# First group of heads taken in pairs, with TensorE's order there written out

## The chip, the cores and the metric

The kernel runs on one core of one Trainium2 chip. The metric is device microseconds (us) of one execution; the median of three runs of the kernel before is 717.41 us (717.05 to 717.48).

## The reference, cut to what matters

Causal attention with a bias from cumulative sums, then a mixture of four experts over every token, then a gated feed-forward layer. All inputs are fp32.

```
scores = q k^T / 8 ;  cum = cumsum(max(s, 0))
scores = where(causal, -1e9, scores + min(cum_k - cum_q, 0))
attn = exp(scores - max) ;  x = (attn @ v) / (sum(attn) + 1e-9)      # 2 batches, 8 heads, 576 rows, 64 wide
p = probs / (sum(probs) + 1e-9) ;  y = sum_e p_e * relu(x @ w1_e) @ w2_e   # 1152 tokens, 512 wide, 4 experts, 1024 inner
out = ((y @ w_a) * (y @ w_b)) @ w_out                                 # 1536 inner
```

## The kernel before, in words

Attention is cut into four groups of query rows, each over all eight heads. The **first group** is the first 256 rows of batch 0 and runs alone at the start, in plain fp32, by the functions `head_scores`, `head_softmax`, `head_turn`, `head_av` and `pair_out`. Its output, turned so that model columns lie on partitions (`x32`, four pieces, one for each pair of heads), feeds the first matmuls of the first expert (`ps1`, line L1055, made of four products each, one for each piece). From there on TensorE mixes expert matmuls with the attention of groups two to four (jobs; their score matmuls are lines L631 and L632, their transposes L674).

In the first group q and k of an even head lie on partitions 0 to 63 and those of the odd head on 64 to 127 (tile `qk`); the bias rows (`cb`, a rounded part in 8 rows and its remainder 32 rows further on) are kept twice, from partition 0 and from partition 64. So the score matmuls of an even head use array rows 0 to 63 and those of an odd head rows 64 to 127. The scores of a head are two blocks, 128 queries over 128 keys and 128 queries over 256 keys; each block is a bias product (`one`, `rows`) and a q k product in one PSUM tile `sc`, of which there are two. Then VectorE (DVE) takes the minimum and writes `e` (five buffers of tag "e"; the first three of them hold `s_sb`, `ones` and `dif` of the cumulative sums at the start), ScalarE (ACT) exponentiates, TensorE turns `e` in three transposes into `tr`, ACT (even heads) or DVE (odd heads) copies that to `eT`, TensorE multiplies by v with a column of ones (`av`, one tile for a pair), DVE divides (`l`, `r`, `xq`), TensorE turns the pair's result (`xT`), and ACT writes `x32` and `xh`, GpSimd (POOL) `xl`.

The order of instructions on an engine is the scheduler's, except where `in_order` fixes it. `keep_warm(n)` issues n filler matmuls (bf16, 128x512, tile `lull`) with a fixed place. The first job's q, k and v are prepared by `prep_job` behind the third pair (`gate`): ACT writes `qh` and `ks` (L597, L602), SyncE's queue (SP) copies the upper half of `ks` into `kb` by DMA (L603), and POOL writes the remainder into the lower half of `ks` (L605). POOL also forms the experts' shares from `pr`, which SP loads late (`den`, L906 and L908).

Of the kernel before, what the change touches and what calls it, by code (L numbers as in the profile page):

```python
# [8 lines left out]
F32 = mybir.dt.float32  # L9
# [8 lines left out]
B, H, S, D = 2, 8, 576, 64  # L18
E, DM, F1, F2 = 4, 512, 1024, 1536
NT = B * S  # L20
P = 128
# [31 lines left out]
NB = 32 + H  # L53
NS = 64 + NB
# [5 lines left out]
def fused_kernel(ctx, tc, qk0, v0, qT, kT, v, s, dp, w1, w2, wa, wb, wo, out):  # L60
    nc = tc.nc
# [13 lines left out]
    ident = const.tile([P, P], F32, name="ident")  # L75
# [458 lines left out]
    ps_s = actx.enter_context(tc.tile_pool(name="ps_s", bufs=2, space=PSUM))  # L534
# [19 lines left out]
    def in_order(ins):  # L554
        return tc.keep_in_program_order(ins)

    qk = slab.tile([P, H // 2, 2, NT0], F32, tag="wh", name="qk")
# [9 lines left out]
    cb = slab.tile([NS, NT0], F32R, tag="wl", name="cb")  # L567
# [169 lines left out]
    def keep_warm(n):  # L737

        for _ in range(n):
            in_order(nc.tensor.matmul(lull_ps, lhsT=lull[:, :P], rhs=lull, start=True, stop=True))  # L740

    sc = e_p.tile([NS, S], F32, tag="e", name="s_sb")
# [4 lines left out]
    sel = fix_p.tile([NS, H], F32R, name="sel")  # L747
# [34 lines left out]
    in_order(nc.vector.tensor_scalar(  # L782
        out=cb, in0=cum[:NS, :NT0], scalar1=1.0, scalar2=1.0, op0=ALU.mult, op1=ALU.mult
    ))
    for lo_, eng in ((slice(32, NB), nc.vector), (slice(96, NS), nc.gpsimd)):
        in_order(eng.tensor_tensor(
            out=cb[lo_], in0=cum[lo_, :NT0], in1=cb[lo_].bitcast(F32), op=ALU.subtract
        ))
    nc.gpsimd.memset(v65[:, :, :, D : D + 1], 1.0)

    K0 = 3 * P
    heads = {}

    def head_scores(h):
        a = (h % 2) * D
        q, k = (qk[a : a + D, h // 2, i] for i in range(2))
        one, rows = sel[a : a + NB, h : h + 1].broadcast_to([NB, P]), cb[a : a + NB]
        ps = ps_s.tile([P, K0], F32, tag="sc", name=f"sc{h}")
        heads[h] = {"ps": ps}
        for n0, n1, q0 in ((0, P, 0), (P, K0, P)):  # L800
            nc.tensor.matmul(
                ps[:, n0:n1], lhsT=one, rhs=rows[:, : n1 - n0], start=True, stop=False
            )
            nc.tensor.matmul(  # L804
                ps[:, n0:n1], lhsT=q[:, q0 : q0 + P], rhs=k[:, : n1 - n0], start=False, stop=True
            )
        if h % 2:
            keep_warm(1)

    def head_softmax(h):  # L810
        ps = heads[h]["ps"]
        e = heads[h]["e"] = e_p.tile([P, K0], F32, tag="e", name=f"e{h}")
        mn = st_p.tile([P, 2], F32, tag="mn", name="mn")
        for i, (n0, n1) in enumerate(((0, P), (P, K0))):
            nc.vector.tensor_tensor_reduce(
                out=e[:, n0:n1], in0=ps[:, n0:n1], in1=causal[:, S - n1 + n0 :],
                scale=-SCALE, scalar=3.0e38, op0=ALU.add, op1=ALU.min, accum_out=mn[:, i : i + 1],
            )
            nc.scalar.activation(
                out=e[:, n0:n1], in_=e[:, n0:n1], func=AF.Exp, bias=mn[:, i : i + 1], scale=-1.0  # L820
            )

    def head_turn(h):
        e = heads[h]["e"]
        ps = ps_t.tile([P, 3, P], F32, tag="tr", name=f"tr{h}")
        for i in range(3):
            nc.tensor.transpose(ps[:, i, :], e[:, i * P : i * P + P], ident)
        eT = heads[h]["eT"] = et_p.tile([P, 3, P], F32, tag="eh", name=f"eT{h}")
        if h % 2:
            nc.vector.tensor_copy(out=eT, in_=ps)  # L830
        else:
            nc.scalar.activation(out=eT, in_=ps, func=AF.Copy)

    def head_av(h):
        eT = heads[h]["eT"]
        if h % 2 == 0:
            heads["av"] = ps_m.tile([P, 2, 2, VW], F32, tag="mm", name="av0")
        av = heads["av"]
        for t, i, c, first_, last in ((0, 0, 0, True, True), (1, 1, 0, True, False), (1, 2, 1, False, True)):
            nc.tensor.matmul(  # L840
                av[:, t, h % 2, : D + 1], lhsT=eT[:, i, :], rhs=v65[:, c, h, : D + 1],
                start=first_, stop=last,
            )
        if h % 2:
            keep_warm(1)

    last = []

    def pair_out(j):
        av = heads["av"]  # L850
        l, r = (st_p.tile([P, 2, 2], F32, tag=t, name=t) for t in "lr")
        nc.vector.tensor_scalar(out=l, in0=av[:, :, :, D], scalar1=1e-9, scalar2=None, op0=ALU.add)
        nc.vector.reciprocal(out=r, in_=l)
        xq = x_p.tile([P, 2, 2, D], F32, tag=("xs", "xt")[j % 2], name="xq")
        x = nc.vector.tensor_tensor(
            out=xq, in0=av[:, :, :, :D], in1=r.unsqueeze(3).broadcast_to([P, 2, 2, D]), op=ALU.mult
        )
        ps = ps_a.tile([P, NT0], F32, tag="av", name="xT")
        for t in range(2):
            nc.tensor.transpose(  # L860
                ps[:, t * P : t * P + P], xq[:, t].rearrange("p a d -> p (a d)"), ident
            )
        y = nc.scalar.activation(out=x32[j], in_=ps, func=AF.Copy)
        last.append((x.ins, y.ins))
        nc.scalar.activation(out=xh[j][:, :NT0], in_=ps, func=AF.Copy)
        nc.gpsimd.tensor_tensor(
            out=xl[j][:, :NT0], in0=x32[j], in1=xh[j][:, :NT0].bitcast(F32), op=ALU.subtract
        )
# [42 lines left out]
        for e in range(E):  # L911
            nc.gpsimd.tensor_tensor(out=pr[:, :, e], in0=pr[:, :, e], in1=den, op=ALU.mult)

    for h in range(H + 3):
        if h < H:
            head_scores(h)
        if h == 0:
            sums_of_s()
        if h < H:
            head_softmax(h)  # L920
        if 0 <= h - 2 < H:
            head_turn(h - 2)
        if 0 <= h - 3 < H:
            head_av(h - 3)
            if (h - 3) % 2:
                pair_out((h - 3) // 2)

    jobs = [make_job(gi, h) for gi in range(1, len(GROUPS)) for h in range(H)]

# [4 lines left out]
    def at(n):  # L934
        return seq[n] if 0 <= n < len(seq) else None
# [364 lines left out]
    for n in range(len(seq) + 12):  # L1300
        x = at(n)
# [108 lines left out]
```

## Time and profile before

| what | value |
|---|---|
| median of three runs | 717.41 us |
| the profiled execution: its own time | 716.52 us |
| the profiled execution: span of its instructions | 714.8 us |
| PE busy / DVE / ACT / POOL in that span | 707.0 / 500.2 / 334.0 / 419.7 us |

The span runs from the first to the last instruction of the trace; 1.7 us of the execution lie outside it. A busy PE in this profile has modelled ends, so the starts of its instructions tell more than its share.

### The profile page before, as it was taken

What the parts mean: (1) busy time and instruction counts of PE and PEld (TensorE: products, weight loads), DVE (VectorE), ACT (ScalarE), POOL (GpSimd) and SP (SyncE); (2) the same over time, 40 slices, a digit from 0 to 9 for tenths busy, and PEclk for the clock granted to TensorE, in tenths of its full rate; (3) what the DMA queues carried; (4) which work ended last, traced back from release to release, by engine and by line L of the source; (5) the groups of instructions that cost most, each with busy time, mean ns of one, the idle gap of its engine ahead of it and who ended that gap; (6) DMA issues with size and microseconds to landing.
All of it is one profiled execution on the core that took longest, in us unless ns stands there. A gap on an engine that the chain in (4) does not pass through costs nothing.

```text
span 714.8 us, 11136 instructions
## 1 busy us (share of the span) xinstructions
PE 707.0 (99%) x3892; PEld 621.7 (87%) x3892; DVE 500.2 (70%) x1039; ACT 334.0 (47%) x734; POOL 419.7 (59%) x421
## 2 busy tenths in 40 slices
PE   9999999999999999999999999999999999999998
PEld 5877899999999988888888888887999899989886
DVE  5567978877769576667666666588976557875672
ACT  3568969988743333333333223434543544423410
POOL 5476876766623564444344357578275898878700
PEclk9999999999999999999999999999999999999999
DMA  8665742454211121222111131222021322222002
GB/s 327 202 192 151 224 129 84 107 142 113 74 59 41 60 88 37 68 62 71 53 53 56 47 88 61 88 87 91 30 72 47 98 82 88 86 66 85 30 30 104
DMA packets 34877, 65.63 MB, mean 92 GB/s; under 512 B 3413, under 2 KB 17653, under 8 KB 34821
## 3 DMA queue, kind: packets, MB, share of 16 engines
q1 hardware_dynamic: 34341, 63.81, 28.7%
q10 hardware_dynamic: 480, 1.11, 0.4%
q8 instruction: 31, 0.51, 0.3%
q14 instruction: 25, 0.20, 0.1%
HBM read 59.31 MB, written 2.58 MB: 87 GB/s over the span
## 4 chain that ended last, share of the span: by engine, by line
PE 89%; POOL 3%; DVE 3%; DMA 2%; ACT 2%; issue 1%; ACTq 0%; DVEq 0%; POOLq 0%
PE ps L284 39%; PE psq L284 30%; PE pst L284 6%; PE ps L1055 3%; PE av L706 3%; PE tr L674 3%; POOL wl L84 2%; PE sc L632 1%; PE sc L631 1%; PE sc L804 1%; PE av L840 1%; DMA qk<-in_qk 1%; PE psq L1160 1%; POOL tp L165 1%; DMA raw<-in_w 1%
## 5 line engine op out<-in xcount | busy, mean ns | idle before, releaser
L284 PE MATMUL ps<-wh,h2h 128*128 128x512 f32 (+1 forms) x320 | 124.8, 390 | 0.0
L284 PE MATMUL ps<-wl,h2h 128*128 128x512 f32 (+1 forms) x320 | 123.9, 387 | 0.0
L284 PE MATMUL ps<-wh,h2l 128*128 128x512 f32 (+1 forms) x320 | 122.1, 388 | 0.0
L84 POOL TENSOR_TENSOR wl<-raw,wh 128x512 fp32r<-128x512 f32 x48 | 62.2, 1322 | 101.5 <-ACT wh L80 80.7
L338 DVE SCALAR_TENSOR_TENSOR acc<-ps,pr,acc 128x512 f32<-128x512 f32 x105 | 77.6, 746 | 38.5 <-PE ps L284 38.0
L284 PE MATMUL psq<-xh,wh 128*128 128x448 f32 (+1 forms) x224 | 81.5, 365 | 0.8 <-DVE psq L439 0.8
L284 PE MATMUL psq<-xl,wh 128*128 128x448 f32 (+1 forms) x224 | 81.3, 363 | 0.0
L284 PE MATMUL psq<-xh,wl 128*128 128x448 f32 (+1 forms) x224 | 81.3, 364 | 0.0
L349 ACT ACTIVATE h2h<-psq 128x448 fp32r<-128x448 f32 (+1 forms) x56 | 29.7, 531 | 102.5 <-PE psq L284 82.4
L284 PEld LDWEIGHTS ps<-wh,h2l 128*128 128x128 f32 x320 | 60.1, 188 | 12.5
L284 PEld LDWEIGHTS ps<-wh,h2h 128*128 128x128 f32 x320 | 60.2, 188 | 11.1 <-DVE acc L338 0.4
L284 PEld LDWEIGHTS ps<-wl,h2h 128*128 128x128 f32 x320 | 60.1, 188 | 10.7
L84 POOL TENSOR_TENSOR wl<-sums,wh 128x512 fp32r<-128x512 f32 x48 | 62.1, 1317 | 3.9 <-ACT wh L80 3.9
L284 PE MATMUL psq<-tql,wh 128*128 128x448 f32 x144 | 52.7, 366 | 0.0
L284 PE MATMUL psq<-tqh,wl 128*128 128x448 f32 x144 | 52.5, 364 | 0.0
L284 PE MATMUL psq<-tqh,wh 128*128 128x448 f32 x144 | 52.4, 365 | 0.0
L165 POOL TENSOR_SCALAR tp<-tp 128x512 f32<-128x512 f32 x24 | 46.9, 1968 | 5.3 <-ACT tp L164 5.3
L690 DVE TENSOR_TENSOR el<-tr,eh 128x512 fp32r<-128x512 f32 (+5 forms) x80 | 38.6, 485 | 14.0 <-ACT eh L689 12.9
L439 DVE TENSOR_TENSOR u<-psq,s 128x448 f32<-128x448 f32 x44 | 27.3, 620 | 29.8 <-PE psq L284 28.8
L663 POOL TENSOR_SCALAR e<-e,r 128x448 f32<-128x448 f32 (+4 forms) x64 | 37.9, 597 | 16.7 <-DVE r L662 11.4
L284 PEld LDWEIGHTS psq<-xh,wh 128*128 128x128 f32 x224 | 42.1, 188 | 4.7 <-DVE psq L439 1.1
L80 ACT ACTIVATE wh<-raw 128x1024 fp32r<-128x1024 f32 x24 | 25.5, 1062 | 43.6 <-PE ps L284 23.8
(204 smaller groups left out, 1931.5 us busy)
## 6 DMA issues: line engine op xcount, KB each, us to landing
raw<-in_w SPq DMA_DIRECT2D x40, 512.0 KB
raw<-in_wa SPq DMA_DIRECT2D x12, 512.0 KB
raw<-in_wb SPq DMA_DIRECT2D x12, 512.0 KB
raw<-in_wo SPq DMA_DIRECT2D x12, 512.0 KB
kr<-in_kT SPq DMA_DIRECT2D x16, 288.0 KB
w<-in_w SPq DMA_DIRECT2D x8, 512.0 KB
vr<-in_v SPq DMA_DIRECT2D x16, 160.0 KB
kb<-ks SPq DMA_DIRECT2D x16, 144.0 KB
```

The costliest lines, as they stand in the source:

```text
L80: nc.scalar.activation(out=hi, in_=src, func=AF.Copy)
L84: lo_eng.tensor_tensor(out=lo[:, x], in0=src[:, x], in1=hi[:, x].bitcast(F32), op=ALU.subtract)
L165: nc.gpsimd.tensor_scalar(out=t.bitcast(F32), in0=t.bitcast(F32), scalar1=2.0**-15, scalar2=GMAX, op0=ALU.max, op1=ALU.min,)
L284: ins = nc.tensor.matmul(ps, lhsT=l, rhs=r, start=first and k == 0, stop=last and k == 2, skip_group_check=more)
L338: nc.vector.scalar_tensor_tensor(out=dst, in0=ps, scalar=share, in1=dst, op0=ALU.mult, op1=ALU.add)
L349: nc.scalar.activation(out=hh, in_=src, func=AF.Relu)
L439: nc.vector.tensor_tensor(out=out, in0=a, in1=b, op=ALU.add)
L663: nc.gpsimd.tensor_scalar(out=t.e, in0=t.e, scalar1=r, scalar2=1.0, op0=ALU.mult, op1=ALU.mult)
L674: ins = nc.tensor.transpose(ps[:, c - c0, :], t.e[:, k0 : k0 + P], ident)
L690: nc.vector.tensor_tensor(out=j.el[:, c0:c1, x], in0=src, in1=hi.bitcast(F32), op=ALU.subtract)
L706: ins = nc.tensor.matmul(ps[:, o:], lhsT=j.vs[:, c, :], rhs=e[:, c, o:], start=(m == 0), stop=(m == len(mms) - 1),)
L1055: ins = nc.tensor.matmul(ps, lhsT=w, rhs=x, start=start, stop=stop)
```

## The change

`head_scores` now takes a pair of heads. It issues both bias products of a block, then both q k products, so that products of the even and the odd head follow one another on different array rows. Every TensorE instruction of the first group (scores, transposes, `av`, `xT`) is now fixed in program order. The fillers behind each pair's scores and behind each pair's `av` are gone (eight of them); three fillers stand behind the scores of the first pair. `pair_out` is split: `pair_norm` (the division, on DVE) comes right behind the pair's `av`, `pair_out` (the turn) one step later. The remainder of `cb` for odd heads moves from POOL to DVE.

```
-    for lo_, eng in ((slice(32, NB), nc.vector), (slice(96, NS), nc.gpsimd)):
-        in_order(eng.tensor_tensor(
+    for lo_ in (slice(32, NB), slice(96, NS)):
+        in_order(nc.vector.tensor_tensor(
...
-    def head_scores(h):
...
+    def head_scores(j):
+        two = []
+        for h in (2 * j, 2 * j + 1):
...
+            two.append((ps, q, k, one, rows))
         for n0, n1, q0 in ((0, P, 0), (P, K0, P)):
...
-        if h % 2:
-            keep_warm(1)
+            for ps, _, _, one, rows in two:
+                in_order(nc.tensor.matmul(
+                    ps[:, n0:n1], lhsT=one, rhs=rows[:, : n1 - n0], start=True, stop=False
+                ))
+            for ps, q, k, _, _ in two:
+                in_order(nc.tensor.matmul(
+                    ps[:, n0:n1], lhsT=q[:, q0 : q0 + P], rhs=k[:, : n1 - n0], start=False, stop=True
+                ))
...
-    for h in range(H + 3):
-        if h < H:
-            head_scores(h)
-        if h == 0:
+    NH = H // 2
+    for j in range(NH + 1):
+        if j < NH:
+            head_scores(j)
+        if j == 0:
+            keep_warm(3)
             sums_of_s()
-        if h < H:
-            head_softmax(h)
-        if 0 <= h - 2 < H:
-            head_turn(h - 2)
-        if 0 <= h - 3 < H:
-            head_av(h - 3)
-            if (h - 3) % 2:
-                pair_out((h - 3) // 2)
+        if j < NH:
+            head_softmax(2 * j)
+        if j:
+            head_turn(2 * j - 1)
+        if j > 1:
+            pair_out(j - 2)
+        if j < NH:
+            head_softmax(2 * j + 1)
+        if j:
+            head_av(2 * j - 2)
+            head_av(2 * j - 1)
+            pair_norm(j - 1)
+        if j < NH:
+            head_turn(2 * j)
+    pair_out(NH - 1)
```

The order of TensorE (PE) around the second pair, before. The number behind `sc`, `tr`, `e` and `eT` is the head, the rest of a name is a buffer number:

```order
L740 MATMUL lullps_122<-lull_120 128x512
L801 MATMUL sc2_225<-cb_114,sel_128 128x128
L804 MATMUL sc2_225<-qk_112 128x128
L801 MATMUL sc2_225<-cb_114,sel_128 128x256
L804 MATMUL sc2_225<-qk_112 128x256
L827 MATMUL tr0_236<-ident_71,e0_207 128x128 x3
L801 MATMUL sc3_242<-cb_114,sel_128 128x128
L804 MATMUL sc3_242<-qk_112 128x128
L801 MATMUL sc3_242<-cb_114,sel_128 128x256
L804 MATMUL sc3_242<-qk_112 128x256
L740 LDWEIGHTS lull_120
L740 MATMUL lullps_122<-lull_120 128x512
```

The same place on PE in the changed kernel:

```order
L831 MATMUL tr0_227<-ident_71,e0_215 128x128 x3
L806 MATMUL sc2_233<-cb_114,sel_128 128x128
L806 MATMUL sc3_234<-cb_114,sel_128 128x128
L810 MATMUL sc2_233<-qk_112 128x128
L810 MATMUL sc3_234<-qk_112 128x128
L806 MATMUL sc2_233<-cb_114,sel_128 128x256
L806 MATMUL sc3_234<-cb_114,sel_128 128x256
L810 MATMUL sc2_233<-qk_112 128x256
L810 MATMUL sc3_234<-qk_112 128x256
L831 MATMUL tr1_249<-ident_71,e1_221 128x128 x3
L844 MATMUL av0_261<-va_113,eT0_231 128x65 x3
L844 MATMUL av0_261<-va_113,eT1_253 128x65 x3
```

The two heads' scores stand together in turn, and the fillers and the transposes between them are gone.

The end of the first group on PE before, from the third pair's `xT` on (`ps1` are the expert's products, `sc0_0_2_2` and `sc0_0_2_3` the first job's first scores, `xT_416` the last pair's turn):

```order
L860 MATMUL xT_390<-ident_71,xq_388 128x128 x2
L1055 MATMUL ps1_465<-ckr_115,w32_116 128x256 x2
L840 MATMUL av0_402<-va_113,eT7_400 128x65 x3
L740 LDWEIGHTS lull_120
L740 MATMUL lullps_122<-lull_120 128x512
L1055 MATMUL ps1_465<-ckr_115,w32_116 128x256
L1055 MATMUL ps1_494<-ckr_115,w32_116 128x256 x3
L860 MATMUL xT_416<-ident_71,xq_414 128x128 x2
L1055 MATMUL ps1_501<-ckr_115,w32_116 128x256 x3
L631 MATMUL sc0_0_2_2_484<-ks0_0_2_442,qh0_0_2_422 128x320
L631 MATMUL sc0_0_2_3_503<-ks0_0_2_442,qh0_0_2_422 128x448
L632 MATMUL sc0_0_2_2_484<-kb0_0_2_425,qb1_84 128x320
```

The same place on PE in the changed kernel:

```order
L866 MATMUL xT_392<-ident_71,xq_378 128x128 x2
L844 MATMUL av0_398<-va_113,eT6_384 128x65 x3
L1070 MATMUL ps1_460<-ckr_115,w32_116 128x256 x2
L1070 MATMUL ps1_489<-ckr_115,w32_116 128x256 x2
L844 MATMUL av0_398<-va_113,eT7_390 128x65 x3
L1070 MATMUL ps1_460<-ckr_115,w32_116 128x256
L1070 MATMUL ps1_489<-ckr_115,w32_116 128x256
L631 MATMUL sc0_0_2_2_479<-ks0_0_2_437,qh0_0_2_417 128x320
L631 MATMUL sc0_0_2_3_498<-ks0_0_2_437,qh0_0_2_417 128x448
L632 MATMUL sc0_0_2_2_479<-kb0_0_2_420,qb1_84 128x320
L632 MATMUL sc0_0_2_3_498<-kb0_0_2_420,qb1_84 128x448
L866 MATMUL xT_411<-ident_71,xq_409 128x128 x2
```

Both have six products of the expert ahead of the last `xT` (twelve instructions in the trace, two for a product); but in the changed kernel the first job's four score matmuls stand ahead of that `xT`, and the three products of `ps1_496` behind it.

## Rows read from the trace of the kernel before

**Rows 1.** The page's line of TensorE: busy time (share of the span) xinstructions.

```profile
PE 707.0 (99%) x3892; PEld 621.7 (87%) x3892; DVE 500.2 (70%) x1039; ACT 334.0 (47%) x734; POOL 419.7 (59%) x421
```

**Rows 2.** Busy time by stretch (columns are length, busy us by engine, clock, DMA).

```profile
5.60:15.50 9.90, 9.61 (x59) 6.89 (x59) 4.75 (x22) 3.65 (x9) 5.54 (x6) 1.00 1.02 403
```

**Rows 3.** Timeline of PE, head 1 and a filler (start, length, engine, line).

```profile
6.95 0.32 PE L801 MATMUL sc<-cb,sel 40*128 40x128 f32 x1
...
8.03 0.39 PE L740 MATMUL lullps<-lull 128*128 128x512 bf16 x1
8.35 0.32 PE L801 MATMUL sc<-cb,sel 40*128 40x128 f32 x1
```

**Rows 4.** Timeline of PE, 20 to 32 us.

```profile
21.86 0.78 PE L840 MATMUL av<-va,eT 128*128 128x65 f32 x6
22.48 0.49 PE L827 MATMUL tr<-ident,e 128*128 128x128 f32 x3
22.81 0.38 PE L860 MATMUL xT<-ident,xq 128*128 128x128 f32 x2
...
28.50 0.38 PE L860 MATMUL xT<-ident,xq 128*128 128x128 f32 x2
28.71 1.46 PE L1055 MATMUL ps<-ckr,w 128*128 128x256 f32 x6
29.82 0.70 PE L631 MATMUL sc<-ks,qh 128*128 128x320 f32 x2
...
30.72 1.46 PE L1055 MATMUL ps<-ckr,w 128*128 128x256 f32 x6
```

**Rows 5.** Timeline of DVE, the first group (in brackets: idle before, and its releaser).

```profile
4.69 0.42 DVE L786 TENSOR_TENSOR cb<-va,cb 8x256 fp32r<-8x256 f32 x1
...
7.39 0.27 DVE L815 CUSTOM_DVE_ANT_0 e<-sc,causal 128x128 f32<-128x128 f32 x1
...
15.46 0.29 DVE L815 CUSTOM_DVE_ANT_0 e<-sc,causal 128x128 f32<-128x128 f32 x1 [3.15 <-POOL ckr L897]
...
16.02 0.29 DVE L815 CUSTOM_DVE_ANT_0 e<-sc,causal 128x128 f32<-128x128 f32 x1
...
17.32 0.55 DVE L830 COPY eT<-tr 128x384 f32<-128x384 f32 x1
```

**Rows 6.** Timeline of POOL, 4 to 34 us.

```profile
5.62 1.28 POOL L786 TENSOR_TENSOR cb<-va,cb 8x256 fp32r<-8x256 f32 x1
...
23.18 0.21 POOL L906 TENSOR_TENSOR den<-pr 128x9 f32<-128x9 f32 x1 [7.76 <-DMA pr<-in_dp]
...
23.93 1.42 POOL L866 TENSOR_TENSOR xl<-ckr,xh 128x256 fp32r<-128x256 f32 x2
...
27.05 1.55 POOL L605 TENSOR_TENSOR ks<-kr,ks 64x288 fp32r<-64x288 f32 x2 [0.30 <-POOL xl L866]
```

**Rows 7.** Timeline of SP's queue and of ACT: a DMA's issue, its reader.

```profile
27.59 0.52 SPq L590 DMA_DIRECT2D qr<-in_qT  x1
...
30.17 0.53 ACT L597 ACTIVATE qh<-qr 128x384 fp32r<-128x384 f32 x1 [0.24 <-DMA qr<-in_qT]
```

**Rows 8.** Busy time by stretch, 26 to 28 us (columns as in rows 2).

```profile
26.00:27.00 1.00, 1.00 (x10) 0.95 (x9) 0.62 (x1) 0.91 (x2) 0.73 (x1) 1.00 0.96 393
27.00:28.00 1.00, 1.00 (x6) 0.90 (x5) 0.93 (x5) 0.00 (x0) 0.95 (x2) 1.00 0.19 78
```

**Rows 9.** Timeline of PE, around its longest wait behind the first group.

```profile
82.75 0.38 PE L284 MATMUL ps<-xh,wh 128*128 128x256 f32 x1 [1.30 <-DVE hl L318]
82.97 0.28 PE L284 MATMUL ps<-xl,wh 128*128 128x256 f32 x1
83.09 0.28 PE L284 MATMUL ps<-xh,wl 128*128 128x256 f32 x1
```

**Rows 10.** Timeline of PE's weight loads, the fillers at the start.

```profile
3.91 0.15 PEld L740 LDWEIGHTS <-lull 128*128 128x128 bf16 x1 [0.28 <-issue]
4.34 0.82 PEld L740 LDWEIGHTS <-lull 128*128 128x128 bf16 x4 [0.28 <-issue]
```

More of the change, by code (lines that the diff above doesn't have):

```diff
@@ L792, in fused_kernel @@
     heads = {}
-    def head_scores(h):
[L795 to L799, printed above, removed]
-        for n0, n1, q0 in ((0, P, 0), (P, K0, P)):
[L801 to L806, printed above, removed]
-        if h % 2:
-            keep_warm(1)
+    def head_scores(j):
+        two = []
+        for h in (2 * j, 2 * j + 1):
+            a = (h % 2) * D
+            q, k = (qk[a : a + D, j, i] for i in range(2))
+            one, rows = sel[a : a + NB, h : h + 1].broadcast_to([NB, P]), cb[a : a + NB]
+            ps = ps_s.tile([P, K0], F32, tag="sc", name=f"sc{h}")
+            heads[h] = {"ps": ps}
+            two.append((ps, q, k, one, rows))
+        for n0, n1, q0 in ((0, P, 0), (P, K0, P)):
+            for ps, _, _, one, rows in two:
[6 more added lines that the diff above has]
+                ))
     def head_softmax(h):
@@ L826, in head_turn @@
         for i in range(3):
-            nc.tensor.transpose(ps[:, i, :], e[:, i * P : i * P + P], ident)
+            in_order(nc.tensor.transpose(ps[:, i, :], e[:, i * P : i * P + P], ident))
         eT = heads[h]["eT"] = et_p.tile([P, 3, P], F32, tag="eh", name=f"eT{h}")
@@ L839, in head_av, with pair_norm @@
         for t, i, c, first_, last in ((0, 0, 0, True, True), (1, 1, 0, True, False), (1, 2, 1, False, True)):
-            nc.tensor.matmul(
+            in_order(nc.tensor.matmul(
                 av[:, t, h % 2, : D + 1], lhsT=eT[:, i, :], rhs=v65[:, c, h, : D + 1],
                 start=first_, stop=last,
-            )
-        if h % 2:
-            keep_warm(1)
+            ))
     last = []
-    def pair_out(j):
+    def pair_norm(j):
         av = heads["av"]
@@ L857, in pair_out @@
         )
+        heads["x", j] = (x, xq)
+    def pair_out(j):
+        x, xq = heads["x", j]
         ps = ps_a.tile([P, NT0], F32, tag="av", name="xT")
         for t in range(2):
-            nc.tensor.transpose(
+            in_order(nc.tensor.transpose(
                 ps[:, t * P : t * P + P], xq[:, t].rearrange("p a d -> p (a d)"), ident
-            )
+            ))
         y = nc.scalar.activation(out=x32[j], in_=ps, func=AF.Copy)
```

## The prediction

> **What bounds the kernel now.** I read the page's line of engines first: TensorE (PE) is busy 707.0 of 714.8 us, the next engine 500.2 [rows 1]. So time can come only from PE's idle, from work that PE need not do, or from work that it does faster. The change touches PE up to the end of the first group alone; behind it the order of PE's instructions is the same list as before. So I looked for the row where both kernels have done the same PE work: the one after the last `xT`, six expert instructions and the first job's four score matmuls (two L631, two L632). In the kernel before that is 30.72 [rows 4]. PE is nearly full from there on, so what the change wins or loses at this point carries to the end, unless a later wait absorbs it.
>
> Then the timelines of that stretch. Between 5.60 and 15.50 PE counts as busy 9.61 of 9.90 us [rows 2], but that count holds modelled ends and fillers. From one start to the next, a head's four score instructions take 6.95 to 8.03, 1.08 us, and a filler 0.32 [rows 3]; a head's `av` takes 0.62 and its three transposes 0.33 (21.86, 22.48, 22.81), the last `xT` 0.21, six expert instructions 1.11 (28.71 to 29.82), and the four score products behind them 0.90 [rows 4]. DVE has a stall of 3.15 us in front of head 4's softmax, released by POOL at 15.46 [rows 5]. POOL is the engine to watch at the end of the group: it waits 7.76 us for the load of `pr`, forms `den` from 23.18, two `xl` from 23.93 (0.71 each), and ends with two L605 from 27.05, 1.55 together [rows 6]. L631 reads what L605 writes.
>
> **The change part by part.**
>
> *Fillers.* Eight go, three come: 5 x 0.32 = 1.6 us less of PE's issue [rows 3]. Some of those eight only filled waits, so 1.6 is an upper bound and 0 the lower.
>
> *Scores in turn.* A pair took 2 x 1.08 = 2.16 us [rows 3]. Nowhere in this trace do products of different array rows follow each other directly in a pair, so the price is unknown. The upper bound is serial: 0.32 + 0.76 a head, less one of the two exits to a full-array instruction, and I call that 2.0 (an estimate: the two heads with no other instruction between). The lower bound is one head's length, 1.08, with a little for issue: 1.2. The four pairs thus save between 0.6 and 3.8 us of PE time. I carry both ends and 1.5 between them. The page "TensorE: Matmul & The Clock Gate" of the Trainium skill, Part 3 (row/col tiling), says that matmuls on different row groups run at once and that weights load beside a running matmul only if the row group differs; by it the pair would be near 1.2. No row here shows this; by the sum below the end is the same at either price.
>
> *Remainder of `cb`.* DVE gets another instruction like the one at 4.69, 0.42 us [rows 5]; POOL loses one of 1.28 that began at 5.62 [rows 6], so that the odd head no longer waits for POOL until 6.9. DVE works without a gap towards head 0's softmax at 7.39 [rows 5], so that comes at about 7.8. With the exponentials behind it the first transposes come at about 8.9. Ahead of them PE has a pair of scores from 5.6 and three fillers (to 8.6 if serial, 7.8 if overlapped): an idle of up to 1.1 us where the kernel before had the next head's scores.
>
> *Order fixed in pairs.* PE now waits at each transposition for its own softmax. DVE needs 0.56 a head (15.46 to 16.02) and 0.55 for an `eT` copy [rows 5]. Walking the new order by hand with these durations, PE reaches:
>
> | PE comes to | serial 2.0 | half 1.5 | full 1.2 |
> |---|---|---|---|
> | the third pair's scores | 13.7 | 13.3 | 13.0 |
> | the transposes of head 5 | 20.1 | 19.1 | 18.8 |
> | the last `av` (head 7) | 25.7 | 24.8 | 24.5 |
> | L631, behind twelve expert instructions | 27.2 | 26.35 | 26.05 |
>
> These are estimates. Their check is simple: work from 5.6 on is 4 x 2.0 + 8 x 0.33 + 8 x 0.62 + 3 x 0.21 + 2 x 1.11 + 3 x 0.32 = 19.4 us if serial, which would end at 25.0; the other 2.2 us are waits for the softmax chain, half of them in the first pair. The softmax that waits for POOL until 15.46 is now that of head 5 instead of head 4 (the buffers' order moves by one), which comes later in the order and then costs little.
>
> *The end of the group.* In the new order the first job's L631 and L632 stand ahead of the last `xT`. So they have to wait for what they read, whatever the first group saved:
> - POOL: `pr` lands when it lands, 23.18, as its load does not depend on PE. From there `den` to 23.93, then three `xl` of 0.71 in place of two, to about 26.1, then L605 with 1.55: 27.65 [rows 6]. So L631 begins at about 27.7.
> - The copy into `kb` (L603, SP's queue). The nearest such transfer goes from its issue at 27.59 to its reader at 30.17, 2.6 us [rows 7]. In the new order it is issued at about 25.3 and shares the engines with the raw loads, which keep them 0.96 busy up to 27 and 0.19 after it [rows 8]. So `kb` is there at about 28.0 to 28.2 and L632 begins then.
> - From 28.50 to 30.72 PE did, in 2.22 us, all that then is left: `xT`, six expert instructions, two L631 and two L632 [rows 4]. By POOL the end is 27.7 + 2.22 = 29.92; by `kb`, with half of the 0.90 of the four score products still to do, it is 28.2 + 0.45 + 0.21 + 1.11 = 29.97.
>
> The sum: 30.72 - 29.95 = 0.77 earlier; I take **0.8**. It is the same for all three columns of the table, since each has PE ready before 27.7 (slack of 0.5 us in the serial one, 1.65 in the fullest).
>
> **Later on.** The only long wait of PE behind the first group that I found is the 1.30 us at 82.75, for DVE's `hl` [rows 9]. That chain begins from a PE product and so shifts along with PE; I cost it at nothing.
>
> **The rivals.**
>
> *The rows do not overlap* (the change doesn't do what it says). Then pairs take 2.0 and the walk ends at 27.2, still inside the cap by POOL. Same time, 716.6. I count it with the forecast.
>
> *The cap does not hold (faster).* If `pr`, `kb` or POOL come earlier, or if L605 goes ahead of an `xl`, then PE goes on from 27.2 (serial) or 26.05 (full) with 2.22 us of work: 29.4 to 28.3, so 1.3 to 2.4 us gained: 716.1 to 715.0. Against it: `pr` released POOL at 23.18 and not PE [rows 6], and its transfer has no part in the change. Chance 0.14, of which half beyond the bound of 0.2%.
>
> *The wait at 82.75 goes (faster).* If the arrangement of DVE's work there shifts by a microsecond, 1.30 us may go [rows 9]; with 0.8 that is 715.3. Nothing in the change moves those instructions. Chance 0.08.
>
> *The clock falls without the fillers (slower).* The change takes fillers out of a stretch where PE waits in several places. At the start of the trace, ahead of full activity, weight loads of fillers are 0.43 apart (3.91 to 4.34) and then 0.82 / 4 = 0.21 [rows 10]: the lower level (1.2 GHz) and the higher (2.4 GHz), work twice as long. If PE fell to the lower one between 8 and 27, each us of work would take two. It has slack of about 0.5, then 0.8 of gain and 1.43 to the bound: from about 2.7 us of work (at full level) done at the lower one the kernel counts as slower, and 3.5 us give 717.41 + 3.5 - 0.5 - 0.8 = 719.6, and 5 us 721.1. The place would be behind the idle ahead of the first transposes, at about 8. Against it: PE stood 1.30 us before 82.75 and its next two products were 0.12 apart (82.97, 83.09), full level for 256 columns at one a cycle [rows 9]. The same page of the Trainium skill, section "HAM oscillation — how this bites in real kernels", says that bursts with waits between them fall back to the lower clock; the wait at 82.75 does not bear that out for one wait of 1.30 us, and no row here has a chain of several. Chance 0.08.
>
> *A second wait like that at 82.75 (slower).* The order at which DVE and ACT take their work shifts, and a job's chain comes late once: 1.3 us [rows 9] against 0.8 gained, 717.9. That is within the bound unless it comes twice. Chance 0.10, of which 0.04 beyond the bound.
>
> **How the numbers follow.** The profiled execution took 716.52 us, of which 714.8 is the span; the median of the runs is 717.41, 0.89 more. I take the gain of 0.8 off the median: 717.41 - 0.8 = **716.6**. 0.2% of this kernel, 1.43 us, is about what a measurement can tell from no change: the forecast's gain lies within it. Forecast with the rows that don't overlap 0.60; cap does not hold 0.14; later wait goes 0.08; clock 0.08; second wait 0.10. Beyond the bound on the fast side: 0.07 + 0.08, and 0.04 for an unnamed gain by a better fit of jobs further on: 0.19. On the slow side: 0.08 + 0.04 = 0.12. The range reaches on the fast side to the full cap-free case, 715.0, and on the slow side to one more wait and some clock, 718.5; outside stand the heavier clock case and a doubled gain, together less than 2 in 10.
>
> **What would show it.** Right: POOL's first L605 near 26.1, the first L631 near 27.7 with PE idle 0.5 to 1.6 us ahead of it, the first L632 near 28.1, the common point near 29.95; a pair of scores of 1.2 to 2.0 us; PE idle near 8; DVE's wait for POOL at head 5. Wrong: L631 ahead of 27 (no cap); expert products or transposes at twice their spacing (clock); the common point right but the end off (a wait further on, to be found as the first place where the two traces' distance changes).

## The result, and the profile after

The changed kernel takes 721.51 us (median of six runs, 719.70 to 723.56) beside 717.42 of the kernel before (717.05 to 717.48): a ratio of 1.0057, with an interval of 1.0040 to 1.0074. The forecast was 716.6 and a range of 715.0 to 718.5, so it is wrong, in sign and size. The changed kernel also scatters over 3.9 us, where these six runs of the old one scatter over 0.4; of 73 later runs of the old one, 71 lie between 716.31 and 718.95 and two, with a mean clock of 0.992, at 722.04 and 722.69; three more, near 729 with a clock of 0.981, count as slow runs and are left out.

The profiled execution, its span and mean granted clock (it took 720.44 us by itself; the one before 716.52):

```profile
core 0: 718.7 us, clock 0.997
```

First the stretch that the forecast is about, in the timeline of PE: a pair's scores, then the end of the first group. They answer to [rows 3] and [rows 4].

```profile
8.60 0.89 PE L831 MATMUL tr<-ident,e 128*128 128x128 f32 x3 [0.65 <-ACT e L823]
...
13.48 0.33 PE L806 MATMUL sc<-cb,sel 40*128 40x128 f32 x2
13.65 0.43 PE L810 MATMUL sc<-qk 64*128 64x128 f32 x4
13.84 0.36 PE L806 MATMUL sc<-cb,sel 40*128 40x256 f32 x2
14.04 0.59 PE L810 MATMUL sc<-qk 64*128 64x256 f32 x4
14.57 0.55 PE L831 MATMUL tr<-ident,e 128*128 128x128 f32 x3
...
25.28 0.78 PE L844 MATMUL av<-va,eT 128*128 128x65 f32 x6
25.89 1.08 PE L1070 MATMUL ps<-ckr,w 128*128 128x256 f32 x4
27.87 0.61 PE L631 MATMUL sc<-ks,qh 128*128 128x320 f32 x2 [0.89 <-POOL ks L605]
29.78 0.59 PE L632 MATMUL sc<-kb,qb 67*128 67x320 f32 x2 [1.29 <-issue]
30.20 0.38 PE L866 MATMUL xT<-ident,xq 128*128 128x128 f32 x2
30.43 1.46 PE L1070 MATMUL ps<-ckr,w 128*128 128x256 f32 x6
31.53 0.50 PE L631 MATMUL sc<-ks,qh 128*128 128x320 f32 x1
```

A pair of heads now takes 13.48 to 14.57, 1.09 us, half of the 2.16 of before: the rows overlap fully. L631 waits for POOL until 27.87 (forecast: 27.7). But L632 begins only at 29.78 (forecast: 28.0 to 28.2), and the common point (the row behind the same PE work in both kernels), which was 30.72, is 31.53: 0.81 later, where 0.77 earlier was expected.

POOL and SP's queue at that place answer to [rows 6] and [rows 7]. The timeline of POOL in the changed kernel:

```profile
26.27 1.54 POOL L605 TENSOR_TENSOR ks<-kr,ks 64x288 fp32r<-64x288 f32 x2
```

and in SP's queue of DMA issues:

```profile
21.50 1.38 SPq L159 DMA_DIRECT2D raw<-in_w  x3
24.75 0.55 SPq L603 DMA_DIRECT2D kb<-ks  x1
```

The same copy in SP's queue in the kernel before:

```profile
26.94 0.55 SPq L603 DMA_DIRECT2D kb<-ks  x1
```

POOL comes to L605 as forecast (26.27, forecast 26.1). The copy into `kb` is issued at 24.75, 2.2 us sooner than before, and its reader begins 5.0 us after. By the semaphore updates that the traces hold, the copy landed at 29.36 in the kernel before, 2.4 us after its issue, and at 29.69 in the changed one, 4.9 us after: issued sooner, it landed later.

Then PE and the clock near 82, which answer to [rows 9]: the timeline of PE,

```profile
79.56 0.31 PE L632 MATMUL sc<-kb,qb 67*128 67x320 f32 x1
82.25 0.39 PE L284 MATMUL ps<-xh,wh 128*128 128x256 f32 x1 [2.38 <-DVE hl L318]
```

and the windows of all engines behind it (start and end, length, busy time and instructions of PE, PEld, DVE, ACT and POOL, and last the granted clock, the DMA share and GB/s):

```profile
82.00:84.00 2.00, 1.75 (x13) 1.75 (x14) 2.00 (x6) 1.10 (x5) 0.00 (x0) 0.87 0.41 137
84.00:86.00 2.00, 2.00 (x10) 1.86 (x10) 1.83 (x7) 1.72 (x5) 0.43 (x1) 0.50 0.94 330
86.00:88.00 2.00, 2.00 (x15) 2.00 (x14) 1.96 (x8) 0.28 (x1) 1.92 (x4) 0.77 0.96 363
88.00:90.00 2.00, 2.00 (x16) 1.84 (x15) 0.00 (x0) 1.95 (x4) 1.52 (x3) 1.00 0.58 149
```

The wait that was 1.30 us is 2.38 us, and behind it the clock falls to 0.50 (the lower level, 1.2 GHz) and is back at 88. Lost to the clock: 0.13, 0.50 and 0.23 of 2 us each, 1.72 us (an estimate from these windows).

The distance between the two traces can be followed on PE at places where both have run the same products, counted by name and shape, fillers left out. Two such places, ahead of this wait and behind it, in the timeline of PE in the kernel before and then in the changed one:

```profile
78.98 0.36 PE L632 MATMUL sc<-kb,qb 67*128 67x448 f32 x1
...
87.32 0.39 PE L284 MATMUL ps<-wh,hl 128*128 128x512 f32 x1
```

```profile
79.21 0.36 PE L632 MATMUL sc<-kb,qb 67*128 67x448 f32 x1
...
90.24 0.39 PE L284 MATMUL ps<-wh,hl 128*128 128x512 f32 x1
```

Of the 0.81 at the common point only 0.23 is left ahead of the wait. The wait (1.08 longer) and the clock (1.72) bring the distance to 2.92; it is 2.67 near 130. The rest of the 3.9 us between the spans comes near 145 (0.45) and near 668 (0.80, where PE waits 1.36 us in place of 0.75). At these two places the kernel before, with nothing but one row of DVE's order moved (the last kernel of the experiments), loses 0.44 and 0.33 as well, so this part is not shown to be the change's.

What DVE does ahead of this `hl`, in the timeline of DVE, in the kernel before and then in the changed one:

```profile
77.34 1.41 DVE L230 TENSOR_TENSOR wl<-raw,wh 128x512 fp32r<-128x512 f32 x2 [0.17 <-ACT wh L228]
78.67 0.41 DVE L318 SCALAR_TENSOR_TENSOR hl<-ps,hh 128x256 fp32r<-128x256 f32 x1
...
80.04 2.26 DVE L230 TENSOR_TENSOR wl<-raw,wh 128x512 fp32r<-128x512 f32 x2
82.30 0.40 DVE L318 SCALAR_TENSOR_TENSOR hl<-ps,hh 128x256 fp32r<-128x256 f32 x1
```

```profile
78.48 3.39 DVE L230 TENSOR_TENSOR wl<-raw,wh 128x512 fp32r<-128x512 f32 x2 [0.63 <-ACT wh L228]
81.79 0.41 DVE L318 SCALAR_TENSOR_TENSOR hl<-ps,hh 128x256 fp32r<-128x256 f32 x1
```

The timeline of POOL in the changed kernel at the same time:

```profile
78.35 2.97 POOL L230 TENSOR_TENSOR wl<-raw,wh 128x512 fp32r<-128x512 f32 x2
```

Before, an `hl` at 78.67 lets PE run one more tile of twelve products (1.4 us) ahead of the wait, which is for the next `hl` at 82.30. In the changed kernel already the first of these `hl` comes only at 81.79, behind a pair of `wl` that starts 1.1 us later and takes 3.39 us beside POOL's pair. The reason stands in DVE's order. Rows of before, then of the changed kernel (`wl_1164` is the piece called `wl_1169` before, `wl_832` is `wl_837`):

```
L230 TENSOR_TENSOR wl_837<-raw_843,wh_836 128x512 x2
L318 SCALAR_TENSOR_TENSOR hl_1075<-ps1_1035,hh_1074 128x256
...
L230 TENSOR_TENSOR wl_1169<-raw_1355,wh_1168 128x512 x2

L230 TENSOR_TENSOR wl_1164<-raw_1350,wh_1163 128x512 x2
L318 SCALAR_TENSOR_TENSOR hl_1070<-ps1_1030,hh_1069 128x256
...
L230 TENSOR_TENSOR wl_832<-raw_838,wh_831 128x512 x2
```

Two weight pieces have changed places, 50 us behind the code that was edited. They are not alone: of some 3,700 TensorE instructions behind the first group about 250 stand at another place than before, the last of them about a tenth of the way in; on ACT and DVE 94 each, on POOL and SP about 20 each.

### The profile page after: what moved, and what is told of

The parts are those of the page before. It is cut to its first block, busy times and chain, and to the rows that moved or that the text cites. A ratio compares the mean times of both kernels' runs of the same rounds, so it can differ in the third digit from the quotient of the medians.

```text
span 718.7 us, 11132 instructions
## 1 busy us (share of the span) xinstructions
PE 704.7 (98%) x3887; PEld 619.8 (86%) x3887; DVE 500.0 (70%) x1040; ACT 333.4 (46%) x734; POOL 419.7 (58%) x420
## 3 DMA queue, kind: packets, MB, share of 16 engines
q10 hardware_dynamic: 480, 1.11, 0.4%
## 4 chain that ended last, share of the span: by engine, by line
PE 74%; POOL 10%; DVE 8%; ACT 4%; DMA 2%; issue 2%; POOLq 0%; DVEq 0%; ACTq 0%; SPq 0%
PE ps L284 34%; PE psq L284 23%; POOL wl L84 5%; PE pst L284 4%; PE ps L1070 3%; PE av L706 3%; PE tr L674 3%; POOL tp L165 2%; DVE tp L173 1%; PE sc L631 1%; PE sc L632 1%; DVE tp L177 1%; DVE tp L169 1%; ACT wh L228 1%; POOL sums L192 1%
## 5 line engine op out<-in xcount | busy, mean ns | idle before, releaser
L284 PEld LDWEIGHTS psq<-xl,wh 128*128 128x128 f32 x224 | 42.1, 188 | 3.6
```

The source lines that it names most:

```text
L284: ins = nc.tensor.matmul(ps, lhsT=l, rhs=r, start=first and k == 0, stop=last and k == 2, skip_group_check=more)
```

## The experiments

All ratios are against runs of the kernel before on the same chip; the medians of these are 717.69, 717.49, 717.27 and 717.09 on the four chips used.

**The two places where PE waits.** Four kernels tell apart the order of the weight pieces, `kb`, the alternation and the clock.

*The pieces in order.* Each conversion of a weight piece is queued behind the last one on ACT, and likewise on DVE:

```
-                nc.scalar.activation(out=wh[:, two, :], in_=r, func=AF.Copy)
...
+                with gated(split_act[-1:]):
+                    split_act.append(nc.scalar.activation(out=wh[:, two, :], in_=r, func=AF.Copy).ins)
+            with gated(split_dve[-1:] if lo_eng is nc.vector else ()):
+                for m in (2 * j, 2 * j + 1):
...
+            if lo_eng is nc.vector:
+                split_dve.append(lo.ins)
```

> The changed kernel, with the conversions of weight pieces (ACT's rounded part, DVE's remainder) held in the order in which they are loaded, which is the order of the kernel before. Theory (the loss has two places: the score products of the first job wait for kb at 29.8, and two weight pieces that changed places on ACT and DVE make PE wait 2.38 us near 82, after which the clock falls): the wait near 82 comes down under 1.5 us, the granted clock stays 1.00 from 80 to 90, the runs lie within 0.5 us of each other, the first group still ends 0.8 late, and the time is 718.0 to 719.0. Rival (the missing fillers and the timing of the first group make the wait and the fall of the clock): a wait of 2 us or more stays, the clock falls, 720 to 723.

Measured: 720.74 (718.50 to 723.17), ratio 1.0048 (1.0031 to 1.0065). The theory falls in this form, and what the rival named came out: a wait of 2.31 us, a falling clock, a time over 720 (whether the first group as such makes them is answered further on, by the exchange of group and order). The wait near 82 is gone, but another one of the same length stands 5 us further on, and in the profiled execution (the slowest of the six) the clock fell at both places, at the end of the first group too, where PE waits 1.55 us for `ks` and 1.30 for `kb`. Its timeline of PE at the two places, then the window behind the first:

```profile
28.23 0.61 PE L636 MATMUL sc<-ks,qh 128*128 128x320 f32 x2 [1.55 <-POOL ks L610]
30.14 0.98 PE L637 MATMUL sc<-kb,qb 67*128 67x320 f32 x2 [1.30 <-issue]
...
87.15 0.64 PE L679 MATMUL tr<-ident,e 128*128 128x128 f32 x2 [2.31 <-DVE r L667]
```

```profile
30.00:35.00 5.00, 4.86 (x14) 4.07 (x15) 2.14 (x6) 3.41 (x10) 2.29 (x4) 0.50 0.21 61
```

The single run whose mean clock was 1.000 took 718.50, the one with 0.993 took 723.17. The four between them stand in the order of their clocks too (0.998: 720.03 and 720.16; 0.995: 721.32 and 722.44), so here the scatter goes with the clock.

*Raw loads behind `kb`.*

```
-    for _ in range(3):
-        load_next()
     gate.extend(last[-2])
     with gated(gate):
         prep_job(jobs[0])
         load_job(jobs[1])
+    for _ in range(3):
+        load_next()
```

> The changed kernel, with the three loads of raw weights on SyncE's queue put behind the copy into kb and the next job's loads. Theory (kb is late because the raw loads fill the DMA engines): first L632 right behind the two L631, near 28.4 in place of 29.78; xT, six expert instructions and four score products done near 30.1 in place of 31.53. The order of the weight pieces is that of the kernel before here, so no fall of the clock: 716.3 to 717.4. Rival (kb's copy takes 5 us for a reason of its own): L632 still at 29.4 or later, and 718 or more.

Measured: 719.48 (717.82 to 721.59), ratio 1.0034 (1.0020 to 1.0048). About `kb` the theory holds, about the time it does not. Its timeline of PE:

```profile
27.59 0.62 PE L631 MATMUL sc<-ks,qh 128*128 128x320 f32 x2 [0.83 <-POOL ks L605]
28.04 0.51 PE L632 MATMUL sc<-kb,qb 67*128 67x320 f32 x2
...
29.72 0.50 PE L631 MATMUL sc<-ks,qh 128*128 128x320 f32 x1
...
38.09 0.59 PE L632 MATMUL sc<-kb,qb 67*128 67x320 f32 x2 [1.44 <-DMA vr<-in_v]
```

With no raw loads in flight L632 follows L631 without a wait, and the common point is 29.72, 1.0 earlier than before and 0.2 earlier than forecast. Its copy into `kb`, issued at 24.53, landed 2.4 us later, where beside the raw loads it took 4.9. Yet the kernel is slower: the raw loads now stand in front of later jobs' transfers (a wait of 1.44 at 38.09), so that PE, 1.0 ahead of the kernel before at the common point, is 1.3 behind it at 42; and the order behind the group is again another one. The clock was 1.000 in four of the seven runs and 0.995 to 0.998 in the others, which the theory did not expect. The profiled execution is the quickest of the seven (717.82).

*Scores by head.* With the pieces in order as in the first kernel, and:

```
-        for n0, n1, q0 in ((0, P, 0), (P, K0, P)):
-            for ps, _, _, one, rows in two:
+        for ps, q, k, one, rows in two:
+            for n0, n1, q0 in ((0, P, 0), (P, K0, P)):
                 in_order(nc.tensor.matmul(
...
-            for ps, q, k, _, _ in two:
                 in_order(nc.tensor.matmul(
```

> As the kernel with the weight pieces in order, but the four score products of the even head stand ahead of those of the odd head, so no two neighbours use different array rows (but for one place in a pair). Theory (pairs overlap nearly fully, but the wait for kb swallows what this gives): a pair takes 1.9 to 2.1 us in place of 1.09, the first L631 begins 0 to 1 us later than 27.9, the first L632 still at 29.8, the time within 0.4 us of the kernel with the pieces in order. Rival (TensorE's order sets the end of the first group): up to 3.6 us slower.

Measured: 723.80 (722.86 to 723.98), ratio 1.0085 (1.0072 to 1.0098). Both numbers of the theory missed: a pair takes 1.41 us (9.69 to 11.10), because the odd head's first products overlap the even head's last ones without any alternation; and L632 waited until 31.07, 6.1 us after the issue of its copy (24.95). The time is 3.06 above the kernel with the pieces in order, inside the rival's range (up to 3.6). But all four runs have a clock under 1.000 (0.993 to 0.998), and the two profiled executions, both with the clock fallen at the end of the group and near 88, differ by 0.81 alone. What TensorE's order in a pair is worth is not settled by this run.

*The kernel before with a longer wait.* DVE writes one half of one piece's remainder three times, and the next `hl` is held behind it:

```
-            for m in (2 * j, 2 * j + 1):
+            for m in (2 * j, *[2 * j + 1] * (3 if nsplit[0] == 8 else 1)):
...
+            if nsplit[0] == 8:
+                again.append(lo.ins)
...
+        with gated(again):
```

> The kernel before, in which DVE computes one piece of a weight remainder three times in place of once, near 80 us; the first group is untouched, all fillers are there. Theory (a wait of 2 us and more on PE takes the clock down for some us, whatever went before): the wait at 82.75 grows from 1.30 to 2.5 to 4 us, the granted clock falls below 1.00 behind it, the runs spread by over 1 us, and the time is 1.2 to 2 us longer than the wait alone makes it: 719.5 to 722. Rival (the clock falls for want of the fillers in the first group): the wait grows but the clock stays 1.00, 718.5 to 720 with a spread under 0.5 us.

Measured: 719.57 (718.28 to 720.43), ratio 1.0026 (1.0015 to 1.0036). The mean clock was 0.998 in five of the seven runs and 1.000 in the two quickest (718.28 and 718.52); the group with all its fillers is untouched, and the wait came out at 2.10, under the 2.5 expected. The timeline of PE at the wait, then the window behind it:

```profile
83.89 0.39 PE L287 MATMUL ps<-xh,wh 128*128 128x256 f32 x1 [2.10 <-DVE hl L322]
```

```profile
84.00:88.00 4.00, 4.00 (x21) 4.00 (x22) 3.23 (x12) 1.78 (x4) 3.82 (x6) 0.58 0.96 304
```

So this longer wait alone is enough for the clock to fall, in most runs though not in all. Between the medians of those two groups of runs lie some 1.5 us (719.86 and 718.40).

**Is it the end of the first group, the fillers, or what comes after?**

*Scores behind the last `xT`.* The first job's score products are issued a step later and behind the eighth product of the first expert:

```
-        if x := at(n):
+        if n == 1:
+            with gated(pe_last[8-1:8]):
+                for i in range(1):
+                    st_scores(*at(i))
+        if n >= 1 and (x := at(n)):
             st_scores(*x)
...
+        pe_last.append(ins.ins)
```

> The changed kernel, with the first job's four score products put behind the last xT and behind eight of the first expert's products in place of ahead of them, so that TensorE has work while kb is on its way. Theory (the two waits at the end of the first group, for POOL's ks and for kb, cost time and in many runs bring the clock down): no wait over 0.7 us between 26 and 31, the clock 1.00 there, the same products done about 1 us earlier than in the kernel before, the weight pieces in their old order, a wait of 1.5 us at most near 82, and 716.2 to 717.6. Rival (the time is lost further on, whatever the end of the first group does): waits of 2 us stay and the time is 719 or more.

Measured: 720.57 (719.03 to 722.17), ratio 1.0044 (1.0032 to 1.0056): the rival's time, though no wait of 2 us stayed (the one near 84 is 1.11) and the profiled execution, the quickest of the five (719.03), had a clock of 1.000. No wait is left between 26 and 31, but there is one of 0.99 at 32.43, and two more came up that the kernel before does not have, in its timeline of PE:

```profile
73.32 0.39 PE L632 MATMUL sc<-ks,qh 128*128 128x256 f32 x1 [1.34 <-DVE mn L643]
...
113.95 0.41 PE L632 MATMUL sc<-ks,qh 128*128 128x320 f32 x1 [1.04 <-DVE mn L643]
```

*Fillers back.*

```
             head_scores(j)
+            keep_warm(3 if j == 0 else 1)
         if j == 0:
-            keep_warm(3)
...
+        if j:
+            keep_warm(2)
```

> The changed kernel with fillers put back behind every pair's scores (one) and behind every pair's av (two). Theory (the clock falls behind the waits of 1.3 us and more, and those stay): the first L631 and L632 wait as before, the wait near 82 is 2 us or more since the weight pieces stand in the changed order here too, the clock falls in most runs, 720 to 723 with a spread over 1 us. Rival (the clock falls for want of fillers): clock 1.00 in all runs, under 719.

Measured: 720.56 (718.76 to 721.21), ratio 1.0043 (1.0030 to 1.0056). From 28 us on TensorE's order is, by names and shapes, that of the changed kernel; the wait near 82 is 2.36. The mean clock stayed 1.000 in three of five runs, which neither theory said, and those three took 718.76 to 720.70: time is lost at full clock too. By its time the theory holds, by the clock neither.

*The kernel before without its fillers.* Nothing else is changed:

```
-        if h % 2:
-            keep_warm(1)
...
-        if h % 2:
-            keep_warm(1)
```

> The kernel before without the eight fillers of the first group, nothing else changed by hand. The scheduler then puts the weight pieces of the changed kernel's order on ACT and DVE. Theory: the first group is no slower, the wait near 82 grows to 2 us or more and the clock falls behind it in most runs: 718.5 to 720.5. Rival (the order of the pieces does not matter, the loss is at the end of the first group): 716.8 to 717.8 with a clock of 1.00.

Measured: 720.30 (718.86 to 728.21), ratio 1.0046 (1.0023 to 1.0070). The theory holds: ten of twelve runs have a clock under 1.000, two of them far under (0.990 at 724.40, 0.986 at 728.21). This is 2.8 of the change's 4.1 us, from two removed lines. And the first group became quicker: its common point is at 30.22, 0.50 ahead of [rows 4]. Its timeline of PE, there and near 82:

```profile
30.22 1.46 PE L1051 MATMUL ps<-ckr,w 128*128 128x256 f32 x6
...
81.84 0.39 PE L284 MATMUL ps<-xh,wh 128*128 128x256 f32 x1 [2.35 <-DVE hl L318]
```

From 52 us on TensorE's order is here, by names and shapes, exactly that of the changed kernel.

**Group and order exchanged.** Each kernel's own code, with edges that hold every engine to a written list (one in ORDER for each of the five) for what is traced behind the first group:

```
+    for order in ORDER.values():
+        row = [by_name[f"I-{at0 + k}"] for k in order]
+        for a_, b_ in zip(row, row[1:]):
+            tc.add_manual_dep(b_, a_.name, NOSYNC, reason="order")
```

> The changed kernel, with everything traced behind the first group issued on each engine in exactly the order of the kernel before (for the first 480 instructions of TensorE, 160 of DVE, 165 of ACT, 90 of POOL, 80 of SyncE; behind these both kernels have one order). Theory (the loss is the scheduler's other order behind the first group): one wait of about 1.3 us near 82 and none over 1 us elsewhere up to 130, clock 1.00, 716.4 to 717.7. Rival (the first group as such, its fillers or its alternating products, makes the loss): 719 or more.

> The kernel before, its first group and fillers untouched, with everything behind it issued in exactly the order of the changed kernel. Theory (the order makes the loss): a wait of 2 us or more near 82, the clock falls behind it in most runs, 719.5 to 722. Rival (the first group makes the loss): 717 to 718 with a clock of 1.00.

Measured: the new group in the old order 717.24 (716.15 to 718.72), ratio 1.0000 (0.9991 to 1.0009). The old group in the new order 720.02 (719.42 to 721.26), ratio 1.0040 (1.0027 to 1.0053). The theory holds on both sides. The timeline of PE, new group in the old order and then old group in the new order:

```profile
28.23 0.70 PE L639 MATMUL sc<-ks,qh 128*128 128x320 f32 x2
29.46 0.63 PE L640 MATMUL sc<-kb,qb 67*128 67x320 f32 x2 [0.53 <-DMA kb<-ks]
29.93 1.46 PE L1078 MATMUL ps<-ckr,w 128*128 128x256 f32 x6
...
81.81 0.39 PE L292 MATMUL ps<-xh,wh 128*128 128x256 f32 x1 [0.95 <-DVE hl L326]
```

```profile
82.01 0.39 PE L292 MATMUL ps<-xh,wh 128*128 128x256 f32 x1 [2.35 <-DVE hl L326]
```

With the order held, the common point moves from 30.72 to 29.93, 0.79 earlier, and the first product behind the wait from 82.75 to 81.81. In the second the profiled execution had a clock of 1.000 and still took 720.0: the order alone costs some 2.7 us beside the 717.27 of that chip, without the clock. Three of its five runs had a clock of 0.998.

*One row moved.* As the new group in the old order, and in DVE's list the `hl` for which PE waits near 82 ahead of the pair of `wl`:

```
-    'DVE': [... 825, 939, 940, 763, 724, 639, ...]
+    'DVE': [... 825, 724, 939, 940, 763, 639, ...]
```

> As the new group in the old order, and one row of DVE's order moved: the hl that PE waits for near 82 stands ahead of the two products of a weight piece's remainder (wl) in place of behind them. Theory (that wait is DVE's order alone): the wait of 1.3 us near 82 goes, 1.0 to 1.4 us faster than the new group in the old order. Rival (another producer is late next): within 0.4 us of it.

Measured: 716.49 (715.46 to 718.77), ratio 0.9991 (0.9981 to 1.0000). The wait is gone (0.26 us at 82.83 is the longest of PE between 31 and 110), and it brought 0.75, between the 1.0 to 1.4 of the theory and the rival's 0.4. Against the kernel before PE gains 1.1 us at the place of the wait and loses 0.75 of it by 97, where the next scores and transposes start later.

In this execution the first group, the same code in the same order, ends otherwise than in the new group in the old order. Its timeline of PE:

```profile
30.34 0.62 PE L640 MATMUL sc<-kb,qb 67*128 67x320 f32 x2 [0.95 <-DMA kb<-ks]
30.80 1.46 PE L1078 MATMUL ps<-ckr,w 128*128 128x256 f32 x6
```

The common point is 30.80, 0.08 later than before, where the execution of the new group in the old order had 29.93. POOL's `den`, which waits for the load of `pr`, begins at 23.95 here and at 23.18 there, and the copy into `kb` landed at 30.29 here and at 29.42 there.

**A better version, and what the group is worth in it.** On TensorE three products of the first expert between L631 and L632, over the transfer of `kb`; in the list of the kernel above; and the kernel before with nothing but the moved `hl`, by the same edit of DVE's list as there:

```
-    'PE': [... 85, 86, 59, 78, 60, 79, 43, 72, 87, 95, ...]
+    'PE': [... 85, 86, 59, 78, 43, 72, 87, 60, 79, 95, ...]
```

> As the kernel with the new group, the old order and hl ahead of wl, and on TensorE three of the first expert's products stand between the first job's two L631 and its two L632 in place of behind them, so that they run while kb is on its way. Theory (kb's arrival, set by the raw loads on the same DMA engines, is the one wait left at the end of the first group): the wait of 0.5 to 0.95 us ahead of the first L632 goes, 0.3 to 0.9 us faster than without it: 715.6 to 716.3. Rival (what PE gains there is absorbed by a later wait): within 0.3 us.

> The kernel before, first group and fillers untouched, its own order behind it, with the one row of DVE's order moved (hl ahead of wl). If the new first group is worth 0.5 to 0.9 us where the order is kept: 0.4 to 0.9 slower than the new group with the same order and row. If the first group is worth nothing: the same within 0.3 us, near 716.4. Against the kernel before it is 0.5 to 1.3 faster on either theory, as the wait of 1.30 us at 82.75 goes.

Measured: 715.54 (714.28 to 716.58), ratio 0.9972 (0.9959 to 0.9986), and 716.41 (715.23 to 717.81), ratio 0.9986 (0.9974 to 0.9999). The first beats both kernels; in its timeline PE has no wait ahead of L640, and one of 0.88 us for DVE behind it:

```profile
27.90 0.70 PE L639 MATMUL sc<-ks,qh 128*128 128x320 f32 x2
28.44 1.46 PE L1078 MATMUL ps<-ckr,w 128*128 128x256 f32 x6
29.55 0.70 PE L640 MATMUL sc<-kb,qb 67*128 67x320 f32 x2
31.13 0.41 PE L639 MATMUL sc<-ks,qh 128*128 128x320 f32 x1 [0.88 <-DVE mn L650]
```

The second is as fast as the new group with the same row moved (716.41 and 716.49, ratios 0.9986 and 0.9991 on two chips): on its own the quicker group is worth nothing that shows. Together with work put over `kb` it is worth 0.9 us (716.41 to 715.54, same chip, twelve runs each; resampling these runs gives 0.1 to 1.5).

## Why the prediction was wrong

**The step that failed** is in its first paragraph: "The change touches PE up to the end of the first group alone; behind it the order of PE's instructions is the same list as before." With it fell "what the change wins or loses at this point carries to the end" and the part "Later on", which cost the wait at 82.75 at nothing. The list is not the same. The scheduler set new orders on all five engines until about 107 us, and the one that it found has a wait of 2.38 us where the old one has 1.30. The exchange of group and order shows that the order makes the loss: the old order takes the new group to 717.24, as fast as before, and the new order takes the old group to 720.02. That is 2.7 of the 4.1 us; the rest shows only where new group and new order stand together, and is not taken apart. The carrying fails by itself too: of the 0.81 at the common point 0.23 was left at 79.

Which row of the new order does the harm is settled only in part. Putting the two weight pieces back removed the wait near 82 and brought another one, but the scheduler set the rest anew as well, so what that swap costs alone is not shown.

Point by point:

- *Fillers*: between 0 and 1.6 us by the forecast; taking them out of the kernel before brought 0.50 at the common point.
- *Scores in turn*: the pair takes 1.09 us, under the lower bound of 1.2. The rule of the Trainium skill that was weighed there ("TensorE: Matmul & The Clock Gate", Part 3, row/col tiling) agrees: products on other rows run at once.
- *Remainder of `cb`*: first transposes at 8.60 (forecast 8.9), a wait of 0.65 ahead of them (up to 1.1). Right.
- *The walk*: third pair's scores at 13.48 (13.0 in the full column), the last `av` at 25.28 (24.5). Too quick by up to 0.8.
- *POOL's cap*: L605 at 26.27 (26.1), L631 at 27.87 (27.7). Right.
- *`kb`*: this term of the sum was mis-sized. The price of 2.6 us was read from a transfer that ran when the raw loads were done [rows 7, 8]; issued sooner, beside them, the copy took 4.9 us to land, and 2.4 without them (raw loads behind `kb`). That made 0.81 later out of 0.77 earlier. Where the order left the six expert instructions and `xT` ahead of L631, as in the kernel before, the common point came 0.79 earlier in one execution and 0.08 later in the next; that the first figure is that of the forecast is luck, as it came about in another order than the forecast's.
- *The rival of the clock* had the mechanism and the wrong place and cause. The want of fillers is not needed for it: the clock was 1.00 through the whole first group of the changed kernel's profile, and it fell in the kernel before with all its fillers, once a wait was made 2.10 us long. Whether fillers make the fall rarer is not settled (with them put back three of five runs kept 1.000, without them none of six). The section "HAM oscillation — how this bites in real kernels" of the Trainium skill ("TensorE: Matmul & The Clock Gate"), which the forecast set aside because one wait of 1.30 us left the clock alone, is borne out by the falls behind waits of 2.10 and 2.38 us, shorter ones than it describes; but the clock stayed at 1.00 behind waits of 2.35 and 2.36 in three profiled executions (fillers back, no fillers, old group in the new order). The chance of 0.08 was too low, for the forecast never asked whether a wait of 1.30 could become one of 2.4.
- *The wait at 82.75 goes* was held unlikely because "Nothing in the change moves those instructions". The change moved them, by the scheduler, and the other way.
- *A second wait like that at 82.75* was priced at one more 1.3 us against a gain; it was the nearest to what came, as a longer wait and with no gain to set against it.

The new group in the old order also shows how 0.8 us at the common point can be gone at the end. Its execution was 0.9 ahead of the profile of before until about 142 us, lost 0.6 near 145 and 0.7 near 664, where PE waits 1.36 us in it and 0.75 in the profile of before; in all other profiled executions PE waits 1.1 us or more there. The profile of before was one of that kernel's quickest (716.52 against a median of 717.42).

## What to carry to other kernels

Where a scheduler sets the order, an edit at the start is an edit of everything behind it: compare the order of all engines to the end before you say that a gain carries, and hold the order by a list when you want to know what the edit itself is worth. A price for a transfer holds only for the traffic it was read in; one that is issued sooner may land no sooner. And a wait that is long already is a risk of its own, as a little more of it can cost the clock as well.

## What the runs showed of the hardware that was not expected

- The clock's fall behind a wait is not certain from run to run: in the kernel before with its wait made longer (2.10 us in the profiled execution) five of seven runs had a mean clock of 0.998 and two had 1.000. In the changed kernel all six runs lay below 1.000 (0.995 to 0.998), but the times do not follow that alone: 0.997 went with 719.70 and 720.44, 0.998 with 721.19 and 721.89. In two executions the clock fell where two waits had only two products between them, of 1.55 and 1.30 us (pieces in order) and of 1.43 and 1.83 us (scores by head); it stayed at 1.00 behind the 0.89 and 1.29 us of the changed kernel.
- Products of two heads overlap without alternation: issued head by head a pair took 1.41 us, in turn 1.09, and apart 2.16.
- Two `wl` on DVE took 1.41 us in the kernel before and 3.39 in the changed one, where POOL's own pair of `wl` ran most of the while (78.35 to 81.32). In the changed kernel the next pair on DVE, at 82.66 with POOL idle, took 1.28; the pair of before at 80.04, the first half of it beside POOL's, took 2.26. No run was made to show the cause.
